# A decode block on Trainium2: two larger VectorE products per K tile, w2 in two column halves, and 192 of w2's rows as half groups

## The chip, the cores and the metric

The kernel runs on one core of one Trainium2 chip. The metric is the device time of one execution, in microseconds (us). The span that a profile shows is some 1.5 us shorter than the time (670.6 and 672.09 us in the profiled run of the changed kernel), because it runs from the first to the last instruction.

## The reference, cut to what matters

The program is one decode step of a transformer block: a layer norm, attention over a cached K and V, a residual, a second layer norm, an MLP with a mish activation, and a second residual.

```python
# B, Sq, D = 4, 1, 640;  H, Sk, Dh = 32, 4096, 128;  F = 1728;  all bfloat16
q = (layernorm(x) @ wq).reshape(B, Sq, H, Dh).transpose(0, 2, 1, 3)
scores = einsum("bhqd,bhkd->bhqk", q, k_cache) * Dh ** -0.5
o = einsum("bhqk,bhkd->bhqd", softmax(scores), v_cache)
h = x + o.transpose(0, 2, 1, 3).reshape(B, Sq, H * Dh) @ wo
m = layernorm(h) @ w1 + b1
h2 = h + (m * tanh(softplus(m))) @ w2
```

The two caches are 268 MB of the 283 MB that are read. The arithmetic is small beside the reading of them.

## The kernel before

The caches are cut into 16 tiles: 4 groups of 8 heads (`hg`), each with 4 batch entries (`b`). A tile's K and its V are 8.4 MB each (128 partitions x 32768 elements), and the program keeps three such slots in SBUF, A, B and C. Within a group K goes to A, B, A, B and V to C, C, A, C.

A K tile passes through a chain, a quarter (`s`) at a time:

1. VectorE multiplies it in place by the query (`mult`).
2. TensorE adds the products up by identity matmuls into one of two PSUM bank pairs (`fold`, 16 matmuls for a quarter). Quarters 0 and 2 share a pair, and so do 1 and 3.
3. VectorE finishes the sum (`reduce`), which frees the bank pair.
4. ScalarE takes the exponential (`exp`).
5. VectorE spreads the result over a head mask (`mask`), and TensorE multiplies the outcome with the V tile (`pv_mm`).

```python
for i in range(NT):                       # VectorE, NT = 16 tiles
    hg, b = divmod(i, N)
    mult(i, 0); mult(i, 1)
    reduce(i, 0)
    mult(i, 2)
    ...                                   # norm of the group before, where b == 0
    reduce(i, 1)
    mult(i, 3)
    reduce(i, 2)
    ...
    reduce(i, 3)
    for s in range(NS): mask(i, s)        # NS = 4 quarters
    if b == N - 1: sums(hg)

for b in (2, 3):                          # TensorE, third and fourth tile of a group
    fold(i + b, 0); fold(i + b, 1); fold(i + b, 2)
    pv_mm(i + b - 1)
    fold(i + b, 3)
    o_mm(i + b - 1)
```

One queue, on SyncE, issues all large loads in order, each when its slot is free:

```python
sp.need(("PV", i - 1));          v_load(i)        # slot C
sp.need(("F", i, NS - 1));       k_load(i + 2)    # slot A, after the last fold of K tile i
sp.need(("PV", i));              v_load(i + 1)    # slot C
sp.need(("F", i + 1, NS - 1));   k_load(i + 3)    # slot B
sp.need(("F", i + 2, NS - 1));   v_load(i + 2)    # slot A, after the last fold of K tile i+2
sp.need(("PV", i + 1));          v_load(i + 3)    # slot C
```

The third V load of each group (`v_load(i + 2)`) waits for the last fold of the third K tile.

After the tiles comes the tail: loads of wo, w1 and w2, the second norm, w1, mish, and w2. In w2, 13 full groups of 128 rows and one of 64 rows are multiplied in four column quarters of 160, at four places of one PSUM bank. Four filler matmuls on zeros run while TensorE waits for the activation.

```python
busy(4)                                   # fillers
pe.need("act")
def w2_mm(j):
    for k in range(CG):                   # CG = 4 quarters, OC = 160 columns
        mm(y2_ps[k * QD : k * QD + N, :], act[0:rows, j, :], w2_sb[:, j, k*OC:(k+1)*OC], ...)
```

The softmax here doesn't subtract the row's maximum and nothing guards it: scores larger than these inputs give would overflow.

## Time and profile before

| | before |
|---|---|
| time, median of 4 runs | 661.59 us (661.48 to 661.71) |
| profiled span, mean granted TensorE clock | 660.0 us, 0.798 |
| busy: VectorE, TensorE | 62%, 58% |
| last byte of the last w2 load lands | 657.57 us |
| from there to the end of the span | 2.47 us |

These lines are from the profile page of the kernel before. The rows DMA and GB/s cut the span into 40 equal slices; DMA is the busy share of the 16 DMA engines in tenths, and the q1 line gives packets, megabytes and the busy share of the 16 engines' span.

```profile
span 660.0 us, 4989 instructions
...
DMA  9999999999999999999999999999999999999997
GB/s 418 409 445 445 438 441 417 422 441 438 438 437 425 429 437 437 441 437 421 433 437 437 441 437 417 437 437 433 441 441 417 437 433 437 441 441 417 425 416 312
...
q1 hardware_dynamic: 6912, 283.35, 99.4%
```

The transfers never stop. So VectorE and TensorE can become slower or faster for a while without any effect on the time, as long as every load is issued before the load ahead of it in the queue has landed. The time that is left between the two is the slack of that load. (A load is issued when SyncE's instruction for it starts; it lands when the DMA engines report their shares of it, one by one, so there is a first and a last landing: in this trace the load of a K or V tile shows 16 landings, spread over 1.2 to 2.0 us.)

These are the VectorE groups of the loop, from the page of the kernel before: line, engine, operation, tiles and shapes, count, then busy us and mean ns of one, then the idle time before them and what ended it.

```profile
L529 DVE TENSOR_TENSOR slotA<-slotA,q_bc 128x8192 bf16<-128x8192 bf16 x32 | 140.7, 4416 | 93.1 <-DMA slotA<-in_A_k_cache_dram 93.1
...
L540 DVE TENSOR_REDUCE s_f<-red 128x64 f32<-128x1024 f32 x64 | 78.0, 1219 | 96.3 <-PE red L740 96.2
...
L554 DVE TENSOR_TENSOR e<-ex,hmask 128x512 bf16<-128x512 bf16 x64 | 39.8, 684 | 0.0
```

The reduces wait 96 us in all for folds (L740 is the fold's line). That wait costs nothing so long as the loads keep their slack.

This is the timeline of VectorE in the third tile of the second group (start, us, what; in brackets the idle time before), and then of SyncE's queue:

```profile
250.67 8.75 DVE L529 TENSOR_TENSOR slotA<-slotA,q_bc 128x8192 bf16<-128x8192 bf16 x2
261.64 1.23 DVE L540 TENSOR_REDUCE s_f<-red 128x64 f32<-128x1024 f32 x1 [2.21 <-PE red L740]
262.78 4.42 DVE L529 TENSOR_TENSOR slotA<-slotA,q_bc 128x8192 bf16<-128x8192 bf16 x1
267.12 1.22 DVE L540 TENSOR_REDUCE s_f<-red 128x64 f32<-128x1024 f32 x1
268.25 4.42 DVE L529 TENSOR_TENSOR slotA<-slotA,q_bc 128x8192 bf16<-128x8192 bf16 x1
272.68 1.23 DVE L540 TENSOR_REDUCE s_f<-red 128x64 f32<-128x1024 f32 x1
279.81 1.23 DVE L540 TENSOR_REDUCE s_f<-red 128x64 f32<-128x1024 f32 x1 [5.90 <-PE red L740]
280.95 2.49 DVE L554 TENSOR_TENSOR e<-ex,hmask 128x512 bf16<-128x512 bf16 x4
```

```profile
279.80 0.33 SPq L263 DMA_DIRECT2D slotA<-in_A_v_cache_dram  x1
```

Products and reduces alternate. The last fold ends at 279.8 us, and in that moment the third V load of the group is issued. The load ahead of it lands from 284.70 us on, so the slack of this load is 4.9 us. In the four groups it is 7.4, 4.9, 5.9 and 7.2 us. (The slacks in this document, like all readings of traces, come from one profiled execution of each kernel.)

This is the end of the timeline of the kernel before. The last 20 w2 matmuls wait for the last w2 load, take 0.62 us, and are copied and stored.

```profile
657.23 0.62 PE L730 MATMUL red<-slotA,act 128*4 128x160 bf16 x20 [0.83 <-DMA slotA<-in_B_w_dram]
657.91 0.32 DVE L726 CAST o_bf<-red 128x160 bf16<-128x160 f32 x1 [3.37 <-PE red L730]
658.26 0.65 SPq L263 DMA_DIRECT2D out_dram<-o_bf  x2
```

### The profile page before, as it was taken

How to read it: one execution, taken by the hardware profiler on the slowest of the kernel's cores; microseconds unless marked ns; L12 is line 12 of the kernel's file. 1: busy time of each engine (PE TensorE's matmuls, PEld its weight loads, DVE VectorE, ACT ScalarE, POOL GpSimd, SP SyncE). 2: the span in 40 equal slices, each digit the busy share in tenths (PEclk: the TensorE clock that was granted, in tenths of full speed). 3: DMA queues.
4: the chain of work that ended last, by engine and by line, in shares of the span. 5: the costliest groups of instructions: out<-in, count | busy, mean ns of one | idle time of the engine just before them, and what ended most of it. 6: DMA issues, size and time to landing. Idle time of an engine off the chain costs nothing. (4 is left out here: it accounts for less than half of the span.)

```text
span 660.0 us, 4989 instructions
## 1 busy us (share of the span) xinstructions
PE 383.8 (58%) x2636; PEld 68.4 (10%) x1680; DVE 407.8 (62%) x257; ACT 40.7 (6%) x157; POOL 1.7 (0%) x12
## 2 busy tenths in 40 slices
PE   1255758457327595838307395838434757665877
PEld 0000100101101010101100010000110001010145
DVE  1087988386048778677219798749206688957612
ACT  0200000000000000000000000000000000000011
POOL 0000000000000000000000000000000000000000
PEclk9778787879659796869668887879876769796868
DMA  9999999999999999999999999999999999999997
GB/s 418 409 445 445 438 441 417 422 441 438 438 437 425 429 437 437 441 437 421 433 437 437 441 437 417 437 437 433 441 441 417 437 433 437 441 441 417 425 416 312
DMA packets 6954, 283.50 MB, mean 430 GB/s; under 512 B 857, under 2 KB 1184, under 8 KB 2208
## 3 DMA queue, kind: packets, MB, share of 16 engines
q1 hardware_dynamic: 6912, 283.35, 99.4%
q8 instruction: 7, 0.11, 0.1%
q14 instruction: 3, 0.02, 0.0%
q10 hardware_dynamic: 32, 0.01, 0.0%
HBM read 283.35 MB, written 0.01 MB: 429 GB/s over the span
## 5 line engine op out<-in xcount | busy, mean ns | idle before, releaser
L529 DVE TENSOR_TENSOR slotA<-slotA,q_bc 128x8192 bf16<-128x8192 bf16 x32 | 140.7, 4416 | 93.1 <-DMA slotA<-in_A_k_cache_dram 93.1
L529 DVE TENSOR_TENSOR slotB<-slotB,q_bc 128x8192 bf16<-128x8192 bf16 x32 | 140.7, 4418 | 18.4 <-DMA slotB<-in_A_k_cache_dram 18.4
L540 DVE TENSOR_REDUCE s_f<-red 128x64 f32<-128x1024 f32 x64 | 78.0, 1219 | 96.3 <-PE red L740 96.2
L740 PE MATMUL red<-slotA,ident 128*128 128x512 bf16 x480 | 135.8, 446 | 0.0
L740 PE MATMUL red<-slotB,ident 128*128 128x512 bf16 x480 | 126.1, 422 | 0.0
L730 PE MATMUL red<-slotA,ident 128*128 128x512 bf16 x32 | 14.7, 458 | 129.4 <-PEq L49 129.4
L730 PE MATMUL pv<-slotC,e 128*32 128x512 bf16 x768 | 51.9, 430 | 37.3 <-PEq L49 34.3
L730 PE MATMUL red<-slotB,ident 128*128 128x512 bf16 x32 | 14.2, 443 | 89.1 <-PEq L49 89.1
L406 ACT ACTIVATE ex<-s_f 128x64 bf16<-128x64 f32 x64 | 16.4, 256 | 513.3 <-DVE s_f L540 513.3
L554 DVE TENSOR_TENSOR e<-ex,hmask 128x512 bf16<-128x512 bf16 x64 | 39.8, 684 | 0.0
L730 PEld LDWEIGHTS pv<-slotC,e 128*32 128x32 bf16 x768 | 22.1, 106 | 95.4 <-issue 81.3
L730 PEld LDWEIGHTS red<-slotA,ident 128*128 128x128 bf16 x32 | 3.2, 99 | 198.0 <-issue 197.9
L730 PEld LDWEIGHTS red<-slotB,ident 128*128 128x128 bf16 x32 | 3.1, 98 | 171.1 <-issue 171.1
L730 PEld LDWEIGHTS o_ps<-pv_sb,selo 128*32 128x32 f32 x136 | 13.5, 109 | 62.6 <-issue 62.6
L730 PE MATMUL o_ps<-pv_sb,selo 128*32 128x128 f32 x136 | 18.0, 276 | 0.0
L730 PE MATMUL pv<-slotA,e 128*32 128x512 bf16 x256 | 14.5, 380 | 0.6 <-PEq L49 0.5
L416 ACT COPY pv_sb<-pv 128x512 f32<-128x512 f32 x16 | 9.4, 586 | 69.5 <-PE pv L730 69.5
L406 ACT ACTIVATION_READ_ACCUMULATOR ex<-s_f 128x1 f32 x64 | 11.9, 186 | 0.0
L730 PEld LDWEIGHTS pv<-slotA,e 128*32 128x32 bf16 x256 | 6.9, 97 | 23.6 <-issue 17.8
L579 DVE RECIPROCAL rl<-misc 32x1 f32<-32x1 f32 x4 | 0.6, 150 | 12.6 <-PE misc L730 12.6
L519 DVE CAST b1T<-pv 128x13 bf16<-128x13 f32 x1 | 0.2, 174 | 12.1 <-PE pv L730 12.1
L730 PE MATMUL y_ps<-a_t,slotB 128*128 128x64 bf16 x160 | 7.3, 211 | 0.0
(107 smaller groups left out, 69.2 us busy)
## 6 DMA issues: line engine op xcount, KB each, us to landing
slotC<-in_A_v_cache_dram SPq DMA_DIRECT2D x2, 4096.0 KB, 42.2
slotC<-in_A_wq_dram SPq DMA_DIRECT2D x1, 5120.0 KB, 15.4
slotB<-in_A_wo_dram SPq DMA_DIRECT2D x3, 1280.0 KB, 15.4
slotA<-in_B_w_dram SPq DMA_DIRECT2D x3, 640.0 KB, 13.9
slotB<-in_B_w_dram SPq DMA_DIRECT2D x2, 864.0 KB, 22.1
slotB<-in_A_wo_dram SPq DMA_DIRECT2D x1, 640.0 KB, 19.0
slotB<-in_A_wo_dram SPq DMA_DIRECT2D x1, 480.0 KB, 19.8
slotB<-in_B_w_dram SPq DMA_DIRECT2D x1, 432.0 KB, 22.8
```

What stands on the lines that cost most here:

```text
L406: lambda: a.activation(out=ex[:, sl], in_=s_f[:, sl], func=ACT.Exp, scale=SCALE, accum_out=rs[:, b, s : s + 1],),
L416: lambda: a.copy(out=pv_sb[:, :, :].rearrange("p r d -> p (r d)"), in_=pv[:, :]),
L519: dv.do(lambda: v.tensor_copy(out=b1T[:, 0:FM], in_=b1_ps[:, 0:FM]), "b1m", DV)
L529: lambda: v.tensor_tensor(out=t, in0=t, in1=q_bc[:, hg, b, :].unsqueeze(1).to_broadcast([P, RS, Dh]), op=ALU.mult,),
L540: lambda: v.tensor_reduce(out=s_f[:, s * RS : (s + 1) * RS], in_=red[:, k : k + 2, :].rearrange("p k (r c) -> p (k r) c", c=CW), axis=AX.X ...
L554: lambda: v.tensor_tensor(out=e[:, sl, :], in0=ex[:, sl].unsqueeze(2).to_broadcast([P, RS, G]), in1=hmask[:, :].unsqueeze(1).to_broadcast( ...
L579: dv.do(lambda: v.reciprocal(out=rl[:, :], in_=l_ps), ("rl", hg), DV)
L730: lambda: nc.tensor.matmul(out_, lhsT=lhsT, rhs=rhs, start=start, stop=stop, skip_group_check=skip),
L740: return t.add_instruction(mybir.InstMatmult(name=nc.get_next_instruction_name(), engine=mybir.EngineType.PE, ins=[t.lower_ap(rhs), t.lowe ...
```

## The change

The intent is a shorter VectorE program and fewer instructions in the tail.

- **Loop.** Four products per tile become two of double size, both ahead of all reduces. Four masks become one, after the last exponential. A fold of quarter 2 or 3 now waits for the exponential that shows its PSUM bank pair is free; before, the order of VectorE's program implied that.
- **w2.** There are 12 full groups, and the last 192 rows go to partitions 0 to 63 as 3 half groups, read in loads of eight partitions with 3840 bytes each (before: 1280). The columns go in two halves of 320 instead of four quarters of 160. VectorE copies one half of the result and ScalarE the other, with one store each.
- **Smaller ones.** The residual is added by fp32 matmuls instead of a high and a low bf16 part; the four fillers before w2 are gone; the norm of a group takes two instructions instead of three; the sums take one instead of two.

The diff; a line of dots marks a cut:

```diff
-    FM = F // P
-    FT = F - FM * P
-    FC = FM + 1
+    FH = 3
+    FT = P // 2
+    FM = (F - FH * FT) // P
+    FC = FM + FH
...
-    OC = D // CG
+    KO = 2
+    OC = D // KO
...
-    y2_ps = red[:, 0, 0:OC]
+    y2_ps = red[:, 0:KO, 0:OC]
...
-            load(sp, w2_tail[r, :], B_w2[FM * P : F, :][r, :], ("w2t", k), "WT")
+            load(
+                sp, w2_tail[r, :, :], B_w2[F0:F, :].rearrange("(p j) n -> p j n", j=FH)[r, :, :],
+                ("w2t", k), "WT",
+            )
...
-            t = slot[KS[b]][:, :].rearrange("p (r d) -> p r d", d=Dh)[:, s * RS : (s + 1) * RS, :]
+            t = slot[KS[b]][:, :].rearrange("p (r d) -> p r d", d=Dh)[:, s * RS : (s + 2) * RS, :]
...
-        def mask(i, s):
-            sl = slice(s * RS, (s + 1) * RS)
-            dv.need(("exp", i, s))
+        def mask(i):
+            dv.need(("exp", i, NS - 1))
...
             mult(i, 0)
-            mult(i, 1)
-            reduce(i, 0)
             mult(i, 2)
             ...                                  # norm
+            reduce(i, 0)
             reduce(i, 1)
-            mult(i, 3)
             reduce(i, 2)
             ...
             reduce(i, 3)
-            for s in range(NS):
-                mask(i, s)
+            mask(i)
...
     def fold(i, s):
-        pe.need(("M", i, s))
+        pe.need(("M", i, s // 2 * 2))
+        if s > 1:
+            pe.need(("exp", i, s - 2))
...
-        busy(4)
         pe.need("act")
...
-            for k in range(CG):
+            for k in range(KO):
                 ...
```

## The prediction

> **What bounds it now.** The transfers. The page's DMA row is 9 in 39 of 40 slices, the queue is busy 99.4%, 283.35 MB move at 430 GB/s. Vector is 62% busy, TensorE 58%; both mostly wait. In steady state one 8.4 MB cache tile takes 19.3 us (between successive landings), a K and V pair 38.6 us. So time is lost only where the queue runs dry, or gained only after the last bytes land (657.2 of 660.0 us in the chain).
>
> How near is dry? I compare each load's issue in the timeline with the landing of the load before it. The tightest is the third V load of each group of four tiles, which reuses the third K tile's slot and so waits for that tile's last fold: it is issued 7.4, 4.9, 5.9 and 7.2 us before the previous load's first landing. The change spends that slack.
>
> **Change in the loop (the large part).** It saves Vector little: four products (4.42 us each) become two of about 8.7; four masks (2.42 together) become one of 2.4; a few small ones go. But it serialises. Before, reduces and folds alternate with products. After, both products (17.4 us) come before any reduce, and the third fold must also wait for the first reduce and its exponential (1.15 + 0.4 us + hand-offs). Then still come fold 3 (3.56 us warm), a PV product (3.57) in three of four tiles, fold 4 (3.56), reduce, exp, and the mask, which can no longer start before the last exp. Replaying the before order with these durations reproduces the issue times from the second group on mostly within 0.5 us. With the new order, a tile takes 32.4 us (was 31.9), then 34.5 (was 28.6), and the third reaches its last fold after 30.0 (was 29.1). These 97 us meet five transfers (96.6 us) that cover them. The slack becomes about 0, and issue to first byte costs 1 to 1.7 us (kernel start), so the queue runs dry once per group, about 2 us each: 5 to 10 us over four groups, central 7, as a late engine loses less.
>
> TensorE's halved clock is inside this: fold pairs after 8 us of idleness took 8.5 to 9.9 us instead of 7.1. [...] the granted clock here changes in steps of 3.41 us. Its phase is unknown, worth about 2 us.
>
> **Change in the tail (small).** Same bytes. The eight-row tail loads grow from 1280 to 3840 B a row. [...] estimated from packet times (55, 149, 196 ns) those get 0.38 us more, the others 0.38 less. [...] +0.4 to +1.5. One store per queue instead of two saves 0.37, the 4x320 copy costs 0.13. Net about +0.8.
>
> **Time.** 661.7 + 7 + 0.8 = 669.5 us, range 664.0 to 674.5. Chances: faster over 2% 0.01, within 2% 0.91, slower over 2% 0.08.
>
> **Right if** the DMA share dips near the third V load of each group (near 130, 287, 444, 601 us), that load is issued at or after the previous landing, and Vector waits for folds longer after its two products. Summed packet time stays.
>
> **Wrong if** folds are warm more often (slack stays positive: 661 to 663 us), cold folds cost more (up to 678), or an instruction fetch hits another engine at the end[...].

## The result, and the profile after

| | before | after | difference |
|---|---|---|---|
| time, median of 4 runs each | 661.59 us | 671.13 us (670.29 to 672.09) | +9.5 |
| ratio, 95% interval | | 1.0145 (1.013 to 1.016) | |
| profiled span, granted clock | 660.0, 0.798 | 670.6, 0.802 | +10.6 |
| last byte of the last w2 load lands | 657.57 | 665.66 | +8.1 |
| from there to the end of the span | 2.47 | 4.99 | +2.5 |

A ratio here and below is the mean time of one kernel's fast runs over the mean of the other's in the same rounds, so it is not quite the ratio of the medians. The profiled run of the changed kernel was its slowest, 672.09 us, so its 10.6 us is a little more than the 9.5 us between the medians. The changed kernel is 1.45% slower, which is still inside the 2% that count as the same.

The page of the changed kernel:

```profile
span 670.6 us, 4865 instructions
...
GB/s 434 430 415 414 434 438 438 431 434 420 427 438 434 426 430 434 438 379 438 438 438 414 430 407 438 438 375 434 430 418 414 434 438 438 438 438 438 407 407 265
...
q1 hardware_dynamic: 6904, 283.35, 98.4%
```

The same megabytes move, but two slices, the 18th and the 27th (16.8 us each, from 285 and from 436 us on), fall to 379 and 375 GB/s. The kernel before has no slice below 409 until its last.

The same VectorE groups of the changed kernel:

```profile
L535 DVE TENSOR_TENSOR slotA<-slotA,q_bc 128x16384 bf16<-128x16384 bf16 x16 | 138.3, 8686 | 99.4 <-DMA slotA<-in_A_k_cache_dram 99.4
L546 DVE TENSOR_REDUCE s_f<-red 128x64 f32<-128x1024 f32 x64 | 77.0, 1219 | 129.6 <-PE red L722 129.5
...
L559 DVE TENSOR_TENSOR e<-ex,hmask 128x2048 bf16<-128x2048 bf16 x16 | 36.7, 2292 | 6.6 <-ACT ex L414 6.6
```

VectorE's work did become shorter: 2.4 us less for slot A's products, 3.1 us less for the masks, and from 407.8 to 402.3 us of busy time in all. But its reduces now wait 129.5 us for folds, 33 us more.

A tile of the changed kernel, the third of the third group, on VectorE and then on SyncE's queue:

```profile
415.97 17.29 DVE L535 TENSOR_TENSOR slotA<-slotA,q_bc 128x16384 bf16<-128x16384 bf16 x2
433.17 1.22 DVE L546 TENSOR_REDUCE s_f<-red 128x64 f32<-128x1024 f32 x1
434.62 1.22 DVE L546 TENSOR_REDUCE s_f<-red 128x64 f32<-128x1024 f32 x1 [0.23 <-PE red L722]
438.57 1.23 DVE L546 TENSOR_REDUCE s_f<-red 128x64 f32<-128x1024 f32 x1 [2.73 <-PE red L722]
445.70 1.22 DVE L546 TENSOR_REDUCE s_f<-red 128x64 f32<-128x1024 f32 x1 [5.90 <-PE red L722]
447.34 2.29 DVE L559 TENSOR_TENSOR e<-ex,hmask 128x2048 bf16<-128x2048 bf16 x1 [0.41 <-ACT ex L414]
```

```profile
445.69 0.33 SPq L261 DMA_DIRECT2D slotA<-in_A_v_cache_dram  x1
```

No reduce comes between the two products. So the first bank pair comes free only at about 434.4 us, and the third and the fourth fold, with the PV product between them, all run after that. The V load is issued 29.7 us after the tile's first product began; before it was 29.1 us. That is not much, but the tile itself also began later: the second V load of the group, which is one tile earlier in the same chain, has lost slack too. Most of the delay is in the second tile of a group: from its first product to that of the third tile it takes 32.8 to 34.2 us, where it took 28.5 to 29.2 us before. The merged mask is a small part: from the start of a tile's last reduce to the end of its masking 3.93 us pass, before 3.63 us. This table gives the time from the issue of a load (in the timeline of the queue) to the first landing of the load ahead of it (in the trace); a negative number means that the load came too late.

| slack, us, in groups 1 to 4 | before | after |
|---|---|---|
| second V load | 9.5, 7.0, 8.0, 6.2 | 4.2, 2.0, 1.1, 4.7 |
| third V load | 7.4, 4.9, 5.9, 7.2 | 1.2, -0.6, -1.2, 2.3 |

The windows view shows what follows in the queue. Its columns are the stretch, its length, the busy us and counts of TensorE matmuls, TensorE weight loads, VectorE, ScalarE and GpSimd, then the granted clock, the DMA share and GB/s. First the kernel before:

```profile
280.00:290.00 10.00, 0.76 (x7) 0.49 (x5) 6.80 (x6) 0.35 (x2) 0.00 (x0) 0.74 0.98 426
440.00:450.00 10.00, 4.25 (x14) 0.10 (x1) 8.76 (x2) 0.00 (x0) 0.00 (x0) 0.57 0.98 426
```

Then the changed kernel:

```profile
280.00:290.00 10.00, 7.72 (x84) 2.26 (x61) 3.68 (x3) 1.28 (x5) 0.00 (x0) 1.00 0.83 334
440.00:450.00 10.00, 6.65 (x64) 1.74 (x41) 3.89 (x3) 1.11 (x5) 0.00 (x0) 1.00 0.78 308
```

The DMA share falls to 0.83 and 0.78 where the third V load is late. I summed two kinds of loss over the trace's DMA packets, as means over the 16 engines.

- **Dry queue.** Engines had nothing to do for 0.5 us near 131, 1.4 us near 287 and 2.1 us near 445 us, and 0.2 us elsewhere: 4.2 us (a recount by the number of packets in flight gives 4.5). The kernel before has none after its start. In the second group SyncE's instruction for the late load ran from 286.76 to 287.09 us, and the load's first packets started at 287.71 us: 0.95 us after the instruction began, 0.62 us after it ended. The load ahead landed from 286.18 to 288.97 us, so its last engines were still at work then. A slack of 1.2 us is already too little: in the first group the queue was dry for 0.5 us.
- **Slow packets.** A 65,536-byte packet usually takes 2.42 us. The first packets of a load that comes onto a dry or nearly dry queue mostly took 2.7 to 3.5 us. Time above the usual sums to 5.1 us (before: 1.2 us), so 3.9 us more. Of the 5.1 us, 3.4 us lie in the stretches around six late loads.

Together they make 8.1 us on the mean engine. The last landing, which is one engine's, came 8.1 us later. That is a check and not an identity, because the engines' lags changed too.

The other 2.5 us are in the tail. This is the end of the timeline of the changed kernel:

```profile
664.46 0.96 PE L712 MATMUL red<-slotB,act 64*4 64x320 bf16 x6 [0.74 <-DVE act L701]
...
665.35 3.37 PE L712 MATMUL red<-slotA,act 128*4 128x320 bf16 x24
668.75 0.48 DVE L708 CAST o_bf<-red 4x320 bf16<-4x320 f32 x1 [4.34 <-PE red L712]
...
669.26 0.30 SPq L261 DMA_DIRECT2D out_dram<-o_bf  x1
```

TensorE starts w2 as soon as the activation is there (664.4 us) and needs 4.3 us for its 30 matmuls, without a wait for any load. It ends 3.1 us after the last landing. In the kernel before, it ended 0.3 us after it. From the end of w2 to the end of the span the change saves 0.3 us (2.2 to 1.9 us).

The windows view of the changed kernel's tail, in steps of 3.41 us, tells why these matmuls are slow (the granted clock is the third column from the right):

```profile
659.02:662.43 3.41, 3.41 (x80) 3.06 (x76) 0.45 (x3) 1.03 (x1) 0.00 (x0) 1.00 1.02 418
662.43:665.84 3.41, 2.67 (x35) 1.43 (x34) 1.58 (x6) 0.25 (x1) 0.00 (x0) 0.50 0.63 248
665.84:669.25 3.41, 2.88 (x22) 1.18 (x18) 0.48 (x1) 0.42 (x1) 0.00 (x0) 0.50 0.00 0
```

They run at half clock. The records of the granted clock hold only 0.5 and 1.0 in both traces, and each stretch between two changes is one to seven times 3.41 us long. By what rule it changes is not shown. The busy share of the profile doesn't tell it: TensorE counted as busy for all of 659.02 to 662.43 us (80 matmuls, nearly all of 64 columns or fewer), and in the next stretch the clock was 0.5. In the kernel before, four fillers stood there (1.49 us for the three from 653.49 us); its clock was 0.5 from 653.37 us and back at 1.0 at 656.78 us, before its last 20 matmuls.

There is a second difference in the tail. In the kernel before, the last w2 load landed 5.7 us after the last part of w1 (651.91 to 657.57 us). In the changed kernel it was 4.7 us (661.00 to 665.66 us): the loads at the end landed closer together (within 1.7 us of each other for the last load, before 2.3 us). So the chain from w1 to the activation had less time behind the transfers. At full clock this cost next to nothing: in the profile of the changed kernel with fillers (below) the distance was 4.8 us, and the end came 2.4 us after the last landing. At half clock it counts: w2 ended 3.1 us after the last landing here, and 1.4 us after it in the first experiment, where the distance was 5.9 us.

### The profile page after: what moved, and what is told of

Same layout as the page of the kernel before. It is cut to its first block, busy times and chain, and to the rows that moved or that the text cites. A ratio compares the mean times of both kernels' runs of the same rounds, so it can differ in the third digit from the quotient of the medians.

```text
span 670.6 us, 4865 instructions
## 1 busy us (share of the span) xinstructions
PE 375.5 (56%) x2627; PEld 70.7 (11%) x1659; DVE 402.3 (60%) x162; ACT 41.3 (6%) x160; POOL 1.9 (0%) x14
## 5 line engine op out<-in xcount | busy, mean ns | idle before, releaser
L535 DVE TENSOR_TENSOR slotA<-slotA,q_bc 128x16384 bf16<-128x16384 bf16 x16 | 138.3, 8686 | 99.4 <-DMA slotA<-in_A_k_cache_dram 99.4
L546 DVE TENSOR_REDUCE s_f<-red 128x64 f32<-128x1024 f32 x64 | 77.0, 1219 | 129.6 <-PE red L722 129.5
L535 DVE TENSOR_TENSOR slotB<-slotB,q_bc 128x16384 bf16<-128x16384 bf16 x16 | 138.3, 8684 | 0.0
L722 PE MATMUL red<-slotA,ident 128*128 128x512 bf16 x480 | 124.3, 417 | 0.0
L722 PE MATMUL red<-slotB,ident 128*128 128x512 bf16 x480 | 123.4, 415 | 0.0
L712 PE MATMUL red<-slotA,ident 128*128 128x512 bf16 x32 | 13.9, 434 | 145.6 <-PEq L49 145.6
L712 PE MATMUL red<-slotB,ident 128*128 128x512 bf16 x32 | 13.9, 434 | 101.5 <-PEq L49 101.5
L559 DVE TENSOR_TENSOR e<-ex,hmask 128x2048 bf16<-128x2048 bf16 x16 | 36.7, 2292 | 6.6 <-ACT ex L414 6.6
L712 PE MATMUL red<-slotC,lnT 128*32 128x512 bf16 x40 | 4.5, 630 | 5.9 <-PEq L49 5.9
L712 PEld LDWEIGHTS y_ps<-a_t,slotB 128*128 128x128 bf16 x160 | 7.0, 131 | 3.9 <-issue 2.9
```

The source lines that it names most:

```text
L535: lambda: v.tensor_tensor(out=t, in0=t, in1=q_bc[:, hg, b, :].unsqueeze(1).to_broadcast([P, 2 * RS, Dh]), op=ALU.mult,),
L546: lambda: v.tensor_reduce(out=s_f[:, s * RS : (s + 1) * RS], in_=red[:, k : k + 2, :].rearrange("p k (r c) -> p (k r) c", c=CW), axis=AX.X ...
L559: lambda: v.tensor_tensor(out=e[:, :, :], in0=ex[:, :].unsqueeze(2).to_broadcast([P, R, G]), in1=hmask[:, :].unsqueeze(1).to_broadcast([P, ...
L712: lambda: nc.tensor.matmul(out_, lhsT=lhsT, rhs=rhs, start=start, stop=stop, skip_group_check=skip),
L722: return t.add_instruction(mybir.InstMatmult(name=nc.get_next_instruction_name(), engine=mybir.EngineType.PE, ins=[t.lower_ap(rhs), t.lowe ...
```

## The experiments

All kernels gave correct results. The theories before them:

- **A, the order of the loop.** Both products ahead of all reduces, and one mask after the last exponential, use up the slack of the V loads. The queue runs dry, and the time is lost there.
- **Rivals.** The tail costs the time (its loads of eight rows, its two column halves, its half clock). Or the long products disturb the transfers themselves: they would make packets slow by their traffic, whatever the slack.

Where an expectation names a theory by a letter, A is the loop's order; its sentence says which rival it sets against it. Some expectations speak of a replay: that is a small estimate of mine that runs the order of the instructions forward with durations measured in the traces, and gives times of issue. Each run was compared with the kernel before on the same chip; those medians were 661.49 to 661.53 us.

| experiment | median us (range) | ratio, 95% interval |
|---|---|---|
| loop back, all else changed | 662.51 (662.13 to 662.65) | 1.0012 (0.9999 to 1.0026) |
| loop only | 671.45 (670.60 to 672.16) | 1.0145 (1.0129 to 1.0160) |
| products and reduces back, one mask | 662.66 (662.55 to 662.74) | 1.0017 (1.0003 to 1.0032) |
| masks early, merged products | 663.18 (662.40 to 664.15) | 1.0023 (1.0008 to 1.0038) |
| products 2, 1, 1 | 699.48 (one run, state unknown) | none |
| changed kernel with fillers | 671.06 (669.58 to 672.19) | 1.0149 (1.0133 to 1.0164) |
| loop back, fillers | 661.54 (661.36 to 661.59) | 0.9999 (0.9985 to 1.0013) |
| loop back, fillers, quarters | 661.68 (661.60 to 661.80) | 1.0003 (0.9989 to 1.0016) |
| kernel before with halves | 661.44 (661.38 to 661.75) | 0.9999 (0.9986 to 1.0013) |
| kernel before with halves, two fillers | 661.56 (661.32 to 662.42) | 1.0002 (0.9989 to 1.0014) |
| masks early, two fillers | 662.74 (662.33 to 665.11) | 1.0030 (1.0017 to 1.0043) |

### Loop back: the changed kernel with the order of products, reduces and masks of before

```diff
             mult(i, 0)
+            mult(i, 1)
+            reduce(i, 0)
             mult(i, 2)
             ...
-            reduce(i, 0)
             reduce(i, 1)
+            mult(i, 3)
             reduce(i, 2)
             ...
             reduce(i, 3)
-            mask(i)
+            for s in range(NS):
+                mask(i, s)
```

Lines that follow from these (the size of a product, the waits of the folds) are left out here and in the next diffs.

> The changed kernel, with only the loop of the before kernel put back: four products, reduces between them, four masks, and the folds' old waits; its tail (column halves, 192 rows on 64 partitions, no filler matmuls before w2) stays. Theory A (the loop order empties the load queue, about 8 of the 9.5 us; the tail costs the rest): 661.9 to 663.5 us, no dip of the DMA share before the tail, third V loads issued 4 to 7 us before the previous landing. Theory B (the tail with its slow TensorE clock is the main loss): stays near 669 to 671 us.

It took 662.51 us, so the loop's order accounts for nearly all of the loss. The slacks of the third V loads are those of before again (7.3, 4.8, 5.7 and 7.0 us), and the queue is never dry. What is left is 1.0 us. The last landing, at 657.90 us, is 0.3 us later than before, and from there to the end 3.3 us pass instead of 2.5. One line of the timeline shows the latter: w2 at half clock, ending 1.4 us after the last landing.

```profile
655.91 3.36 PE L716 MATMUL red<-slotA,act 128*4 128x320 bf16 x24
```

### Loop only: the kernel before with the changed order of the loop

```diff
-            mult(i, 1)
-            reduce(i, 0)
             mult(i, 2)
             ...
+            reduce(i, 0)
             reduce(i, 1)
-            mult(i, 3)
             ...
-            for s in range(NS):
-                mask(i, s)
+            mask(i)
```

> The before kernel with only the new loop (two products, then the reduces, one mask, third and fourth fold waiting for the exponentials). Theory A: 668 to 671 us, with the queue dry near the third V load of two to four groups, and a tail after the last landing of about 2.5 us as before. Theory B (tail): about 661.6 us. If A and the parts add, e1 minus before plus e2 minus before is about the change's 9.5 us.

It took 671.45 us, just above the expected range: the loop alone makes all of the difference. The slacks of the third V loads are 1.8, -0.6, -0.1 and 0.2 us. The queue is dry near 130, 248, 288, 446 and 603 us, 4.1 us in all, and slow packets sum to 7.1 us. The end comes 2.5 us after the last landing, as in the kernel before. So no part of the tail is needed for a loss of this size. Its loop even loses more than the loop of the changed kernel (last landing 668.21 against 665.66 us). The norm of a group, which stays at three instructions here (1.6 us against 1.4 us), is the difference that the replay names; no run tests it.

### Products and reduces back, but one mask

```diff
             mult(i, 0)
+            mult(i, 1)
+            reduce(i, 0)
             mult(i, 2)
             ...
-            reduce(i, 0)
             reduce(i, 1)
+            mult(i, 3)
             reduce(i, 2)
             ...
             mask(i)                     # still one
```

> The changed kernel with the four products, the reduces between them and the folds' old waits put back, but the one merged mask kept. Theory A (one chain, one slack): putting back either piece alone is enough, because the replay gives third V loads issued 4.5 to 5.6 us ahead; so 662.2 to 663.2 us, as with the whole loop put back (662.51), although the early masks alone also sufficed (663.18). If the two pieces cost separately and add, about 2 us should be left: 664 to 666.

It took 662.66 us, like the kernel with the whole loop put back, with slacks of 7.3, 4.8, 5.7 and 3.6 us. So a single mask after the last exponential is not enough to cost anything. And with the mask left as in the changed kernel, the order of products, reduces and fold waits alone takes the time from 671.13 to 662.66 us.

### Masks early, but merged products

```diff
+            for k in range(NS - 1):
+                mask(i, k)              # once the third exponential is there
             reduce(i, 3)
-            mask(i)
+            mask(i, NS - 1)
```

> The changed kernel, merged products kept, but the one mask is split into four again and the first three stand before the last reduce, where Vector waits for the last fold anyway. This shortens a tile by about 1.8 us (three masks of 0.6). Theory A (what counts is the length of the tile's chain against the slack): the replay gives third V loads issued 2 to 3 us ahead instead of 0, so nearly all of the loop's loss comes back: 663 to 665.5 us. Theory C (the merged 16384-element products themselves slow the transfers, whatever the order): no gain, 669 to 672 us.

It took 663.18 us, although the two long products ran ahead of all reduces as in the changed kernel. This is its third tile of the second group on VectorE, then the queue:

```profile
251.63 17.29 DVE L535 TENSOR_TENSOR slotA<-slotA,q_bc 128x16384 bf16<-128x16384 bf16 x2
268.83 1.22 DVE L546 TENSOR_REDUCE s_f<-red 128x64 f32<-128x1024 f32 x1
...
277.88 1.89 DVE L560 TENSOR_TENSOR e<-ex,hmask 128x512 bf16<-128x512 bf16 x3 [2.43 <-PE pv L715]
281.35 1.23 DVE L546 TENSOR_REDUCE s_f<-red 128x64 f32<-128x1024 f32 x1 [1.58 <-PE red L725]
282.99 0.69 DVE L560 TENSOR_TENSOR e<-ex,hmask 128x512 bf16<-128x512 bf16 x1 [0.41 <-ACT ex L414]
```

```profile
281.35 0.33 SPq L261 DMA_DIRECT2D slotA<-in_A_v_cache_dram  x1
```

Three of the masks now run beside the last fold, so only 0.7 us of masking is left after the last exponential (changed kernel: 2.3 us), and the next tile begins earlier. The slacks are 3.9, 3.5, 2.3 and 2.9 us: small, but enough, and the queue is dry for 0.04 us in all. Slow packets sum to 1.3 us, as in the kernel before (1.2 us). This rules out the rival that the long products themselves make packets slow: they are all here, and the slow packets are not. What is left over 661.5 us is mostly the tail again, with w2 at half clock until 660.1 us.

This experiment is not the order of the products alone, with the masks of before. In the kernel before all four masks come after the last reduce; here three come ahead of it. From the start of the last reduce to the end of the masking, a tile takes 3.63 us in the kernel before, 3.93 us with the merged mask and 2.33 us here. So the early masks give back more than the merge had cost, and that new gain hides much of what the long products cost. Merged products with four masks where they were before were not run. Since the merge of the masks costs only 0.3 us per tile, I estimate that they would give back at most 0.6 us of the third V load's slack, which two tiles precede.

### Products 2, 1, 1: the same work in an order that the replay calls bad

```diff
-            mult(i, 0)
-            mult(i, 2)
+            mult(i, 0, 2)               # two quarters in one product
+            reduce(i, 0)
+            mult(i, 2, 1)
             ...
-            reduce(i, 0)
             reduce(i, 1)
+            mult(i, 3, 1)
             reduce(i, 2)
```

> The changed kernel with the loop order nearly back: the first two products stay merged, the third and fourth are single again, and the reduces stand between them as before; the folds wait as before. One Vector instruction fewer per tile than before. Theory A (only the length of the tile's chain against the slack counts): the first fold can start only after the double product, and Vector meets the first reduce at once and idles about 5 us in every tile until that fold is done (a cold fold lasts 5 to 6 us). The replay gives 27 to 35 us of dry queue, plus about 5 us for slow first packets: 690 to 702 us, slower than the changed kernel. Rival (it is the late start of the reduces and the wait for the exponentials that costs, so bringing them forward helps): 662 to 668 us.

It took 699.48 us in its one run, 38 us more than the kernel before, with the same bytes and nearly the same VectorE work. From its page:

```profile
GB/s 417 424 422 470 424 368 421 301 422 418 425 443 443 428 364 424 421 300 421 421 458 443 421 421 361 421 300 421 439 462 421 421 421 417 424 300 413 398 417 289
...
L546 DVE TENSOR_REDUCE s_f<-red 128x64 f32<-128x1024 f32 x64 | 78.1, 1220 | 175.6 <-PE red L723 175.5
```

There are now two holes per group, at the second and the third V load, whose slacks are about -0.8 and -4.4 us. The queue is dry for 30.4 us, and slow packets sum to 7.2 us. Here VectorE waits for the first fold before it makes the third product, and TensorE then waits for that. (In the trace of the kernel before, a single fold took 3.6 us at full clock and 4.9 to 6.4 us where the clock was partly at half.) The expectation had 27 to 35 us of dry queue and about 5 us of slow packets. A theory that gets an order right which was made to be worse is stronger than one that only explains the case it was made from.

### The changed kernel with the four fillers

```diff
+        busy(4)
         pe.need("act")
```

> The changed kernel with the four filler matmuls before w2 put back, as the before kernel has them. In the changed kernel the 24 w2 matmuls took 3.37 us at half the granted clock, after the last landing. Theory A: the clock rises a window earlier, 0.5 to 2 us less: 669.2 to 670.7 us, loop unchanged. If the tail's TensorE time is not on the path: 671 as before.

The median, 671.06 us, did not move. Its profiled run was also its fastest (669.58 us). This is w2 there, to be held against the 3.37 us of the changed kernel:

```profile
664.41 1.79 PE L712 MATMUL red<-slotA,act 128*4 128x320 bf16 x24
```

The end came 2.4 us after the last landing, where the changed kernel needed 5.0 us; the last landing itself was the same (665.73 and 665.66 us). So in this pair of profiles the half clock is worth the tail's whole loss. But here the clock stood at 1.0 from 646.8 us to the end and never fell, so this profile doesn't show the fillers raising it. And the runs spread over 2.6 us, and the clock's phase differs from run to run (its changes at 662.43 us there and at 646.8 us here are 4.6 steps of 3.41 us apart), as do the loop's losses, so the fillers' worth for the median of this kernel stays unclear. In kernels whose loop does not starve, the spread is small enough to see it:

### Loop back, with fillers

```diff
+        busy(4)                         # added to the first experiment's kernel
         pe.need("act")
```

> The before loop with the changed tail (as in the first experiment, which took 662.51), and the four filler matmuls before w2. There the w2 matmuls took 4.3 us to their end, about 1.3 us after the last landing. If the slow clock is most of the tail's 0.9 us: 661.6 to 662.1. If it is the 192 rows alone: 662.4 to 662.6.

It took 661.54 us, 1.0 us less than without the fillers, and the same as the kernel before. One line of its timeline, to be held against the 3.36 us above:

```profile
656.42 1.79 PE L716 MATMUL red<-slotA,act 128*4 128x320 bf16 x24
```

The 24 matmuls are the same; at full clock they end 0.5 us after the last landing. So what the tail costs when the loop is put back is the missing fillers, and the half clock is how they cost it.

### Loop back, with fillers, and w2 in quarters again

```diff
-    KO = 2
+    KO = 4
...                                      # and the copies and stores of before
```

> The before loop, fillers, and w2 again as four column quarters with two stores per queue; of the changed tail only the 192 rows on 64 partitions and small instructions are left. If the rows cost the 0.38 us that packet times give for the engines that take them: 661.8 to 662.2. If the rows cost nothing: 661.5.

It took 661.68 us, between the two expectations (661.5, and 661.8 or more). Only the 192 rows (and the small changes) now differ from the kernel before, whose median was 0.2 us less, and the ratio's interval, 0.9989 to 1.0016, holds 1. The last landing is 0.1 us later than before (657.66 us). My estimate of 0.38 us more on the loaded engines is not shown by this. It came from packet times (in the traces 55 ns for 1280 bytes, 149 ns for 3840 and 196 ns for 5120) and from the assumption that the same eight of the 16 engines take all of the eight-row loads. The trace of the kernel before shows a part of that: each of the four other w2 loads has 16 landings, while the eight loads of eight rows have 64 together, from 650.27 to 653.26 us (and eight further events, each 3.0 us or less after the issue of a load). Which engines took them it doesn't show.

### The kernel before, with halves only

```diff
-    OC = D // CG
+    KO = 2
+    OC = D // KO
...                                      # and one copy and one store for each half
```

> The before kernel with only the two column halves: two wider w2 matmuls per group, the result copied by Vector and Scalar side by side, one store per queue. One store fewer saves 0.37 us, the wider copy costs about 0.13: 661.1 to 661.5 us, and the time from the last landing to the end shrinks by 0.1 to 0.4 us if TensorE's clock is not slower there than before. This would be the version that beats both.

It took 661.44 us: a tie. What the halves save at the copy and the stores is about 0.3 us. But the 320-column matmuls take longer at the end (w2 ends at 658.05 instead of 657.85 us).

### The kernel before, with halves and two fillers

```diff
-        busy(4)
+        busy(2)
```

> The before kernel with column halves as in the last batch (661.44), but two filler matmuls before w2 instead of four. There the four fillers ran until 655.8 while the activations were ready at 654.6, so w2 started 1.1 us late and was still busy 0.5 us after the last landing. With two it starts at about 654.9 and is done with all but the last group when it lands: 661.0 to 661.4 us, if the clock still rises in time; if two fillers are too few for the clock, 661.7 to 662.4.

This was a try at a version that beats both kernels: with fewer fillers w2 can start earlier. It is a tie as well, 661.56 us. In its profiled run, the slowest (662.42 us), the clock stayed at 0.5 until 659.03 us. With two fillers the clock was not back in time in this run.

### Masks early, with two fillers

```diff
+        busy(2)                         # added to the masks-early kernel
```

> The changed kernel with the first three masks early (663.18 with the slow-clock tail) and two fillers before w2: both found losses mended, the merged products kept. If they are the two causes and independent: 661.6 to 662.6 us, that is, equal to the before kernel within its loop's remaining near-dry moments. If the tail's loss has another cause than the clock: 663 again.

It took 662.74 us, just above the expected range, in runs from 662.33 to 665.11 us. The slacks of the third V loads are 4.2, 2.2, 3.1 and 3.5 us in the profiled run. It does not beat the kernel before either, and its two longest runs (664.77 and 665.11 us) suggest that such a small slack is sometimes used up; no profile of those two exists. No version that I ran beats the kernel before.

## Why the prediction was right or wrong

The time was right: 669.5 us was predicted, and 671.13 us measured, inside the range and within 2%. The steps:

- **What bounds the kernel: right.** VectorE became 5.5 us shorter in its busy time and the kernel 9.5 us longer. Only the queue's supply counted.
- **The slack of the third V load: right in kind.** "The slack becomes about 0" held in groups 2 and 3 (-0.6 and -1.2 us). The chain from a group's first product to the issue of this load, predicted at 97 us, took 94.3 to 95.9 us (before: 87.6 to 89.7). Groups 1 and 4 kept 1.2 and 2.3 us, so "issued at or after the previous landing" was wrong there. The first of them was dry anyway, because the load's first packet started 1.0 us after its issue (128.97 to 129.98 us). The dip at 601 us did not come in the profiled run; it did come in the loop-only kernel.
- **The loss in the loop: 7 us predicted, 8.1 us found,** as the shift of the last landing. But "summed packet time stays" was wrong: it grew by 3.9 us, nearly half of the loss. The first packets of a late load are slow, and I had counted only empty time. Of the 7 us of empty queue that I predicted, only 4.2 us were found, so it is luck that the sum came out nearly right.
- **The tail: +0.8 us predicted, +2.5 us found.** This is the term of the sum that was mis-sized. I put it down to loaded engines ("+0.4 to +1.5"), an estimate that rested on which engines take the eight-row loads, and no trace here shows that; the run with the quarters leaves at most some 0.2 us for that. I missed that w2 without fillers ran at half clock, where its 30 matmuls of 320 columns took 4.3 us. Shown: 1.0 us of it, by adding the fillers to the kernel with the loop put back. The rest rests on one pair of profiles, the changed kernel's with and without fillers: 2.6 us less after the last landing at full clock. Half clock costs more there than in the kernel with the loop put back, mainly because the last landing follows sooner after w1's (4.7 us, there 5.9 us). The gain from one store and the copies was 0.3 us (predicted: 0.24 us; VectorE's copy took 0.48 us, before 0.32 us).
- **"Its phase is unknown, worth about 2 us": fits, but no run shows that the phase is the cause.** The changed kernel's four runs spread over 1.8 us, and those of before over 0.2 us.
- **"An instruction fetch" at the end: what it costs is not shown.** The 16 KB packets of the queues marked "instruction" took 0.9 to 1.2 us in the kernel before (the last at 645.55, 653.11 and 656.82 us) and 0.9 to 1.0 us in the changed kernel (the last at 652.01 and 661.51 us).

Open: why the fillers don't move the median of the changed kernel, why the loop alone loses 2.5 us more than the same loop in the changed kernel, and where the diffuse rest of the slow packets comes from. The parts don't add up exactly either (9.9 us for the loop alone and 1.0 us for the rest, against 9.5 us together).

## What to carry to other kernels

In a kernel bound by transfers, look at the slack of each load (its issue against the landing ahead of it), not at an engine's busy time: a program with less work can be slower if it delays the last use of a buffer. Slack hides a delay until it is nearly used up: here 2 to 4 us on the third V load cost almost nothing, and about 1 us ran dry. When you put one part of a change back, check that the experiment doesn't also improve on the old kernel, as the early masks did, or it hides what the other part costs. Merging instructions lengthens the time until the first result of the merged piece (here a product of 8.69 us instead of 4.42 us); leave small instructions where another engine waits for the first part, and keep TensorE on full clock into the last matmuls (here 24 of them took 1.79 us at full and 3.36 us at half clock).
